# Merging halves of an attention block's PV sums in SBUF by VectorE or GpSimd, with the instruction order searched anew

## The chip, the cores and the metric

One Trainium2 chip, one core of it. The metric is the device time of one execution in microseconds (us). The kernel before took 420.92 us, the median of three runs (420.01 to 422.0).

## The reference

The input x has 2048 rows of 448 numbers in bfloat16. With `xn` the layer norm of x, the kernel computes

```python
s = attention(xn)            # qkv = xn @ wqkv, 16 heads of 28, softmax(q k^T / sqrt(28)) v, then @ wo
g = silu(gelu(xn @ w1 + b1) @ w2 + b2)      # 448 -> 1792 -> 448
return x + s * g
```

The largest part is the softmax: 16 heads with 2048 x 2048 scores each, 67 million exponentials.

## The kernel before, in words

**Tiles.** Heads are taken in 4 groups of four, queries in 4 chunks of 512; a group and a chunk make one of 16 blocks. A block has 16 key tiles of 128 and 4 heads, so 64 positions; there are 1024 positions in all. One position is a score matmul of 128 keys by 512 queries into one of the 8 banks of PSUM (`ring`), with 28 + 4 rows of contraction, so that up to four positions stand in the four row groups of the PE array at the same time (`t_score`, L1680). The PV product of one position is a matmul with 32 output columns; four stand side by side (`t_pv`, L2192) and add up in one bank that is held for the block. A set of four side by side is called a step below.

**Two ways to an exponential.** ScalarE (ACT) takes most positions: one ACTIVATE over two neighbouring banks (a pair, 1024 columns) or three (a triple, 1536), L1734. Some groups of four positions, called late groups, go to VectorE (DVE): one multiply-add and a cast to uint16 make a bfloat16 that is a rough exponential (`p_apass`, L2014, four of 512 columns). To make it finer, two shifted copies are derived from the 2048 columns so obtained (`p_expq`): by one 2048-column DVE instruction each (L2087), or by two halves on GpSimd (POOL, L2081). The three together go through PV, the first with the weights `vaug`, the two copies with scaled weights `vs`. So a late group costs 4 + 4 + 4 matmuls of PV, three steps.

**Merging.** Where the tuning says so (MG), the two copies are added first, so that PV needs two steps, not three, and one buffer comes free early. Before, this is an accumulating DMA in SBUF, issued by GpSimd (L2093).

**Beside the softmax.** The projections for K, Q and V and the first MLP product (L124 with the tile `xnT`) are done in PE's spare time; at the middle ACT changes to the gelu (L1570) and back; after it come the second MLP product, tanh for silu (L1607) and the output projection with `wo` (`p_out`, `p_last`). The sums of the softmax go over DRAM to a reciprocal on GpSimd (L2268) or DVE, back by broadcast, and GpSimd scales the block (L2279). Groups of instructions without effect on the output (the tile `zero`, L124) keep PE busy where the plan sees it idle.

**What sets the order.** There is no order written by hand. A planner (`run`, `put`) has generators for all parts, gives each candidate an estimated start from its own table of durations, priorities and due times, and emits the earliest of each engine. Every engine's program is that list, with semaphore waits where a tile needs another engine. 33 numbers per block (`BP`, read by `tune` when a block's scores begin) steer it: among others S4, R3 and JMAX (how many positions a score set takes), MG, GQ and GE (merging), PS and PQ (shifts on GpSimd), LQ and ND4 (late groups in flight). `NQ` bounds the late groups of a block. A small change of a number moves all that comes after it.

Of the kernel before, what the change touches and what calls it, by code (L numbers as in the profile page):

```python
# [8 lines left out]
ALU = mybir.AluOpType  # L9
ET = mybir.EngineType  # L10

PE, ACT, DVE, POOL, SP = ET.PE, ET.Activation, ET.DVE, ET.Pool, ET.SP
# [17 lines left out]
GM = 582  # L30
BPN = ('S4', 'QF', 'MG', 'GQ', 'GE', 'EPS', 'HP', 'JIT', 'RM', 'RG', 'WT', 'PV0', 'PVC', 'MP', 'ND4', 'LU', 'JOINT', 'LQ', 'JMAX', 'DQ', 'URG', 'SLACK', 'UR', 'QLEAD', 'QDIST', 'R3', 'CN', 'CS', 'SR', 'PS', 'PQ', 'BN', 'PVB')
BP = (
# [17 lines left out]
)  # L50
NQ = (14, 3, 13, 4, 5, 11, 15, 16, 8, 15, 8, 9, 8, 11, 8, 10)
QLEAD, QDIST = 0, 12
JMAX, DQ, LQ, ND4, LU = 2, 3, 2, 3, 3
PV0, PVC, MP = 12, 4, 0.3
# [7 lines left out]
MG, GQ, GE = 1, 4.0, 12  # L62
# [3 lines left out]
TXB = 14  # L66
# [3 lines left out]
GP, MP4, GL = 4.64, 1, 1.2  # L70
JIT, RM, RG, HP = 0.01, 0.1, 0.5, 1.15
URG = 12
SPR, AHEAD = 5, 97
R3 = 0
DUE, UR, M0, M2 = 15, 1.25, 59, 981
VT = (15, 14, 13, 12, 11, 10, 9, 8)
SM_SCALE = DH ** -0.5
LOG2E = 1.4426950408889634
# [12 lines left out]
for i in range(ND):  # L91
    k = F0 // ND + (i < F0 % ND)
# [51 lines left out]
class _Kernel:  # L144
# [1685 lines left out]
    def p_late(self):  # L1830
# [6 lines left out]
        for b in range(NBLK):  # L1837
            i = 0
            while True:
                if i:  # L1840
                    K.nq_read = b
                at = 64 * b - QLEAD + (i * (64 - QDIST) // NQ[b] if i else 0)
                yield ("until", lambda: K.next_m >= at)
                K.nq_read = b
                if i >= NQ[b]:
                    break
# [210 lines left out]
    def p_expq(self, m0, u):  # L2057
        K = self
        b = K.sub_of(m0)
        yield ("until", lambda: K.ln2e == 0 and K.a_left[m0] == 0 and K.unit_of(b, 2 if not any(K.sub_of(x) < b for x in K.pend_q) else 4) is not None)  # L2060
        K.ln2e = 1
        K.need -= 1
        K.pend_q.remove(m0)
        us = [u]
        for _ in range(2):
            v = K.unit_of(b, flat=True)
            K.free_u.remove(v)
            us.append(v)
        u16 = dt.uint16
        bT = K.b_U[u]  # L2070
        for i in (1, 2):
            W, T, bW = *K.pair(us[i], u), K.b_U[us[i]]
            if PS in (i, 3) and K.tE[POOL] < K.now + PQ:
                n = (W.shape[1] if len(W.shape) == 3 else 1024) // PH
                for h in range(PH):
                    sl = slice(n * h, n * h + n)

                    def fs(eng, W=W.bitcast(dt.int32), T=T.bitcast(dt.int32), i=i, sl=sl):
                        w, x = (W[:, sl, :], T[:, sl, :]) if len(W.shape) == 3 else (W[:, sl], T[:, sl])
                        k = K.shc[:, i - 1:i] if len(w.shape) == 2 else K.shc[:, i - 1:i, None]  # L2080
                        return eng.tensor_tensor(w, x, k.to_broadcast(list(w.shape)), ALU.add)  # L2081
                    q = slice(4 // PH * h, 4 // PH * h + 4 // PH)
                    yield _Task(POOL, fs, bT[q] + [K.b_shc], bW[q], PD / PH, 0.05, 2, port=True)
                    K.ln2e = 0
                K.ln2e = 0 if i == 2 else 1
                continue
            yield _Task(DVE, lambda eng, W=W, T=T, i=i: eng.tensor_scalar(W.bitcast(u16), T.bitcast(u16), float(SH[i]), None, op0=ALU.add),  # L2087
                        bT, bW, 0.69, 0.0, 4, port=True)
        K.ln2e = 0
        if MG and not {16, 17, 18} & set(us[1:]) and K.next_m < min(64 * (m0 // 64 + 1) - GE, 64 * TXB) and K.tE[POOL] < K.now + GQ and K.smalls <= K.now + 0.5:  # L2090
            v, w = us[1:]
            W, X = K.unit[v], K.unit[w]
            yield _Task(POOL, lambda eng: eng.dma_start(W, X, accum_op=ALU.add), K.b_U[v] + K.b_U[w], K.b_U[v], TXI, TXL, 2, tx=True)  # L2093
            K.free_u.append(w)
            K.n_mg += 1
            K.late_ready.append((m0, ((u, 0), (v, 1))))
            return
        K.late_ready.append((m0, ((us[0], 0), (us[1], 1), (us[2], 1))))
# [298 lines left out]
```

## Time and profile before

| | before |
|---|---|
| median of three runs | 420.92 us |
| the profiled execution, its own time | 418.29 us |
| its span, first to last instruction | 416.5 us |
| outside the span | 1.8 us |
| granted TensorE clock, mean | 0.995 |

The profile is of one execution. Busy time of an engine is the union of its instructions, and consecutive ACTIVATEs overlap at their ends, so that the distance from start to start says more than a duration. In rows of groups, the columns are line, engine, operation, tiles and shape, count, then busy time and mean duration, then the engine's idle time ahead of them and what ended it. DVE is VectorE, ACT is ScalarE, POOL is GpSimd, SP issues most DMAs.

### The profile page before, as it was taken

The page shows a single profiled execution, that of the slowest core. Times are in us where ns is not written, and L with a number is a line of the kernel's source. Part 1 is how long each engine was busy: PE and PEld are TensorE (multiplying, and loading weights), DVE is VectorE, ACT ScalarE, POOL GpSimd, SP SyncE. Part 2 cuts the span into 40 slices and gives each one's busy share as a digit, 9 for nine tenths or more (in the row PEclk, how much of TensorE's full clock was granted, in tenths as well). Part 3 has the DMA queues.
Part 4 walks back from the last instruction along what each step waited for, and adds up shares of the span by engine and source line. Part 5 has one row for each costly group of instructions (what it writes and reads, how often), then busy time and mean ns, then how long its engine had stood idle before and what let it go on. Part 6 is the DMA issues. An engine that isn't in the chain of part 4 may idle for free.

```text
span 416.5 us, 14489 instructions
## 1 busy us (share of the span) xinstructions
PE 396.2 (95%) x6075; PEld 144.2 (35%) x6075; DVE 345.5 (83%) x603; ACT 402.3 (97%) x414; POOL 175.4 (42%) x197
## 2 busy tenths in 40 slices
PE   6999999999999999999999999999999999999994
PEld 4543233333333232222324443332333333222442
DVE  7958978998888978998998117969988979889676
ACT  5899999999999999999999999999999999999994
POOL 7494692304376484113132401048174053164540
PEclk9999999999999999999999999999999999999998
DMA  8701110100101002101330000341200121010172
GB/s 270 266 4 39 4 32 2 32 2 15 31 4 31 5 28 53 33 3 31 88 98 6 28 4 19 64 77 32 54 3 32 31 54 56 20 29 2 27 156 73
DMA packets 18927, 19.12 MB, mean 46 GB/s; under 512 B 8957, under 2 KB 15181, under 8 KB 18830
## 3 DMA queue, kind: packets, MB, share of 16 engines
q1 hardware_dynamic: 17134, 13.44, 11.1%
q0 software_dynamic: 1440, 4.06, 5.4%
q8 instruction: 48, 0.79, 0.7%
q10 hardware_dynamic: 288, 0.69, 0.5%
q14 instruction: 17, 0.14, 0.1%
HBM read 12.54 MB, written 2.88 MB: 37 GB/s over the span
## 4 chain that ended last, share of the span: by engine, by line
PE 68%; ACT 18%; issue 7%; DVE 6%; POOL 1%; ACTq 0%; POOLq 0%; DVEq 0%
PE ring L124 30%; PE ring L1680 18%; PE ring L2192 16%; ACT P L1734 11%; ACT h L1734 4%; ACT xnT L1734 2%; PE ring L1254 1%; DVE vaug L2014 1%; DVE st L997 1%; PE ring L1494 1%; PE ring L1103 1%; DVE h L1618 1%; ACT w L1607 0%; PE ring L1070 0%; PE ring L1185 0%
## 5 line engine op out<-in xcount | busy, mean ns | idle before, releaser
L1734 ACT ACTIVATE P<-ring 128x1024 bf16<-128x1024 f32 (+1 forms) x245 | 251.3, 1136 | 2.2 <-PE ring L1680 1.3
L1680 PE MATMUL ring<-qT,kT 32*128 32x512 bf16 (+2 forms) x1127 | 132.7, 358 | 6.4 <-ACT P L1734 2.6
L1734 ACT ACTIVATE h<-ring 128x1024 bf16<-128x1024 f32 (+1 forms) x82 | 84.2, 1131 | 0.3
L1680 PEld LDWEIGHTS ring<-qT,kT 32*128 32x128 bf16 x1127 | 36.2, 91 | 120.0 <-ACT P L1734 58.6
L2014 DVE TENSOR_SCALAR vaug<-ring 128x512 uint16<-128x512 f32 x88 | 57.8, 683 | 5.7 <-PE ring L1680 5.2
L124 PE MATMUL ring<-xnT,w 128*32 128x512 bf16 x860 | 57.4, 381 | 1.0 <-DVE h L1506 0.6
L124 PE MATMUL ring<-w,h 128*32 128x448 bf16 x896 | 54.4, 355 | 0.5 <-DVE vaug L2014 0.3
L2192 PE MATMUL ring<-P,vaug 128*32 128x512 bf16 (+2 forms) x609 | 51.3, 354 | 0.6 <-ACT xnT L1734 0.3
L2268 POOL TENSOR_TENSOR rc<-rs,mone 128x16 f32<-128x16 bf16 x11 | 33.9, 3086 | 35.0 <-DMA rs<-E_sb 26.5
L2279 POOL TENSOR_TENSOR qT<-x_sb,E_sb 128x512 bf16<-128x512 f32 x15 | 17.8, 1184 | 57.7 <-DMA x_sb<-recs 20.1
L1734 ACT ACTIVATE xnT<-ring 128x1024 bf16<-128x1024 f32 (+2 forms) x33 | 38.4, 1197 | 0.2 <-PE ring L1680 0.2
L2014 DVE TENSOR_SCALAR x_sb<-ring 128x512 uint16<-128x512 f32 x52 | 34.6, 682 | 2.6 <-PE ring L1680 2.4
L124 PEld LDWEIGHTS ring<-xnT,w 128*32 128x32 bf16 x860 | 20.1, 96 | 27.1 <-issue 6.1
L124 PEld LDWEIGHTS ring<-w,h 128*32 128x32 bf16 x896 | 18.5, 95 | 23.0 <-issue 12.4
L1402 POOL TENSOR_TENSOR qsq<-qT 128x512 bf16<-128x512 bf16 x12 | 12.4, 1037 | 30.1 <-DVE qT L1396 28.6
L2192 PE MATMUL ring<-h,vaug 128*32 128x512 bf16 x202 | 22.9, 384 | 0.0
L2014 DVE TENSOR_SCALAR w<-ring 128x512 uint16<-128x512 f32 x32 | 21.2, 682 | 1.0 <-PE ring L1680 0.5
L1121 DVE CAST kT<-ring 128x512 bf16<-128x512 f32 x11 | 7.6, 688 | 16.6 <-PE ring L124 16.6
L2192 PEld LDWEIGHTS ring<-P,vaug 128*32 128x32 bf16 x609 | 14.3, 95 | 14.8 <-issue 8.0
L2014 DVE TENSOR_SCALAR kT<-ring 128x512 uint16<-128x512 f32 x24 | 15.8, 682 | 4.2 <-PE ring L1680 4.2
L2014 DVE TENSOR_SCALAR h<-ring 128x512 uint16<-128x512 f32 x28 | 18.6, 683 | 0.6 <-PE ring L1680 0.4
L1612 POOL TENSOR_TENSOR h<-w 128x448 bf16<-128x448 bf16 x12 | 12.4, 1033 | 15.0 <-PE ring L124 10.0
(235 smaller groups left out, 626.2 us busy)
## 6 DMA issues: line engine op xcount, KB each, us to landing
x_sb<-recs SPq DMA_DIRECT2D x60, 64.0 KB, 2.0
w<-in_B_w_dram SPq DMA_DIRECT2D x1, 1568.0 KB, 7.5
w<-in_B_w_dram SPq DMA_DIRECT2D x1, 1344.0 KB, 8.4
kT<-kT POOLq DMA_DIRECT2D x2, 512.0 KB, 5.5
x_sb<-in_A_x_dram SPq DMA_DIRECT2D x2, 448.0 KB, 4.6
out_dram<-in_A_x_dram SPq DMA_DIRECT2D x2, 448.0 KB, 10.3
out_dram<-h POOLq DMA_DIRECT2D x4, 224.0 KB, 5.1
out_dram<-h SPq DMA_DIRECT2D x8, 112.0 KB, 3.5
```

The costliest lines, as they stand in the source:

```text
L124: ins = eng.matmul(out[q:q + 32, :], w[:, q:q + 32], x, tile_position=(0, q), start=start, stop=stop, skip_group_check=True)
L997: yield _Task(DVE, lambda eng, i=i, t=t: eng.bn_stats(K.st6[:, i, :], K.x_sb[:, c, t, :]), [K.b_x0[h] if c == 0 else K.b_x[c]], [K.b_st[c] ...
L1103: return eng.matmul(bank, w[sl, 3, g * 128:(g + 1) * 128], K.xnT[sl, 3, c * 512:(c + 1) * 512], tile_position=pos, start=False, stop=True, ...
L1121: fn = lambda eng: eng.tensor_copy(dst, bank)
L1402: yield _Task(POOL, lambda eng: eng.tensor_tensor(qs, qb, qb, ALU.mult), [qr], [tq], 1.1, 0.05, 2, port=True)
L1612: yield _Task(POOL, lambda eng, o=o, t=t: eng.tensor_tensor(o, sg[:, t, :], fb[:, t, :], ALU.mult), [K.b_sig[c % 2], K.b_fsb[c % 2]], [K.b ...
L1680: return eng.matmul(dst, K.kT[32 * j:32 * j + 32, g, t * 128:(t + 1) * 128], K.qT[32 * j:32 * j + 32, g, c * 512 + q0:c * 512 + q0 + nq], ...
L1734: return eng.activation(reg[:, i0:i0 + n, :], src, ACTF.Exp, scale=SM_SCALE)
L2014: yield _Task(DVE, lambda eng: eng.tensor_scalar(K.part(u, k).bitcast(dt.uint16), K.like(u, bank), SM_SCALE * LOG2E * 128.0, (127.0 - EXP_ ...
L2192: return eng.matmul(acc[32 * j:32 * j + 32, q0:q0 + nq], w, ap[:, col:col + nq] if len(ap.shape) == 2 else ap[:, col // 128:(col + nq) // ...
L2268: yield _Task(POOL, lambda eng: eng.tensor_tensor(K.rc[:, :], K.rs[:, :], K.mone[:, 0:1].to_broadcast([128, 16]), ALU.pow), [K.b_srs, K.b_ ...
L2279: yield _Task(POOL, lambda eng: eng.tensor_tensor(dst, K.rb, E, ALU.mult), [K.b_rb, tE], [K.b_onT[g][c]], 1.15, 0.05, 1, port=True)
```

## The change

A second branch for merging is put ahead of the old one: for MG = 2 the two copies of a late group are added by one DVE instruction of 2048 columns, for MG above 2 by four GpSimd instructions of 512. The old condition becomes MG == 1. The numbers of the plan are replaced: 16 of the 17 rows of `BP`, `NQ`, `AHEAD`, `M0` and `M2`. In the new rows MG is 2 in one row (the third block's), 1 in seven and 0 in nine; none is above 2.

```diff
-NQ = (14, 3, 13, 4, 5, 11, 15, 16, 8, 15, 8, 9, 8, 11, 8, 10)
+NQ = (14, 4, 4, 4, 7, 10, 15, 16, 8, 15, 11, 9, 5, 9, 8, 10)
...
-SPR, AHEAD = 5, 97
+SPR, AHEAD = 5, 89
...
-DUE, UR, M0, M2 = 15, 1.25, 59, 981
+DUE, UR, M0, M2 = 15, 1.25, 62, 984
...
-        if MG and not {16, 17, 18} & set(us[1:]) and K.next_m < min(64 * (m0 // 64 + 1) - GE, 64 * TXB) and K.tE[POOL] < K.now + GQ and K.smalls <= K.now + 0.5:
+        if MG > 1 and not {16, 17, 18} & set(us[1:]) and K.next_m < 64 * (m0 // 64 + 1) - GE and K.tE[DVE if MG == 2 else POOL] < K.now + GQ:
+            v, w = us[1:]
+            W, X = K.unit[v], K.unit[w]
+            if MG == 2:
+                yield _Task(DVE, lambda eng: eng.tensor_tensor(W, W, X, ALU.add), K.b_U[v] + K.b_U[w], K.b_U[v], 1.15, 0.0, 4, port=True)
+            else:
+                for k in range(4):
+                    yield _Task(POOL, lambda eng, y=K.part(v, k), z=K.part(w, k): eng.tensor_tensor(y, y, z, ALU.add),
+                                [K.b_U[v][k], K.b_U[w][k]], [K.b_U[v][k]], 1.16, 0.05, 2, port=True)
+            K.free_u.append(w)
+            K.n_mg += 1
+            K.late_ready.append((m0, ((u, 0), (v, 1))))
+            return
+        if MG == 1 and not {16, 17, 18} & set(us[1:]) and K.next_m < min(64 * (m0 // 64 + 1) - GE, 64 * TXB) and K.tE[POOL] < K.now + GQ and K.smalls <= K.now + 0.5:
```

Counted in the two programs as they are built (line numbers of the kernel before):

| | before | after |
|---|---|---|
| ACT exponentials: pairs, triples, singles | 298, 61, 1 | 264, 84, 0 |
| late groups | 61 | 61 |
| of these in blocks 0 to 15 | 1 3 6 3 4 2 5 5 3 4 4 5 4 5 5 2 | 1 4 3 3 4 4 4 4 4 4 5 6 4 4 5 2 |
| merges: by DMA, by DVE, by GpSimd | 6, 0, 0 | 3, 2, 0 |
| shifts: DVE of 2048, GpSimd halves | 101, 42 | 92, 60 |
| score sets on PE (one to four positions at once) | 372 | 355 |
| PV matmuls of 512 columns | 1408 | 1412 |
| matmuls of the tile `zero` | 36 | 96 |
| output tiles that take the way over ACT at the end (L2301) | 0 | 1 |

The 17 score sets fewer hold the same number of positions. The first block has the same counts in both.

32 rows, old and new, of the table BP are left out of this document.

## Prediction

> **What bounds the kernel now.** I read the page first, its span and its first part.
>
> ```profile
> span 416.5 us, 14489 instructions
> PE 396.2 (95%) x6075; PEld 144.2 (35%) x6075; DVE 345.5 (83%) x603; ACT 402.3 (97%) x414; POOL 175.4 (42%) x197
> ```
>
> ACT and PE both look full. To tell which one sets the pace I asked for what ACT waits for, and for its busy time in two long stages that hold little but exponentials, with the groups that make them up.
>
> ```profile
> ACT P L1734 <- PE ring L1680: 1.3, 2, 0.8
> ACT P L1734 <- PE ring L2192: 0.4, 1, 0.4
> ACT xnT L1734 <- PE ring L1680: 0.2, 1, 0.2
> ...
> 40.00:220.00 180.00, 179.66 (x186) 1.00 0.12 29
> 252.00:400.00 148.00, 146.47 (x138) 1.00 0.17 38
> ...
> L1734 ACT ACTIVATE P<-ring 128x1024 bf16<-128x1024 f32 x98 | 94.8, 1084 | 0.1
> L1734 ACT ACTIVATE h<-ring 128x1024 bf16<-128x1024 f32 x66 | 65.6, 1080 | 0.1
> L1734 ACT ACTIVATE P<-ring 128x1536 bf16<-128x1536 f32 x12 | 17.9, 1496 | 0.0
> L1734 ACT ACTIVATE h<-ring 128x1536 bf16<-128x1536 f32 x10 | 15.0, 1498 | 0.1
> ```
>
> The first three lines are who ended ACT's waits ahead of exponentials, with the total, the number and the longest: in the whole span 1.9 us, each time PE. The next two are ACT's busy time in 180 and 148 us; the last four are the groups of the first of these stages. The mean durations overstate the cost, as one ACTIVATE begins before the last ends. The distance of starts is in ACT's timeline, in a place without waits.
>
> ```profile
> 119.79 5.61 ACT L1734 ACTIVATE P<-ring 128x1024 bf16<-128x1024 f32 x6
> 125.23 4.75 ACT L1734 ACTIVATE h<-ring 128x1024 bf16<-128x1024 f32 x5
> ...
> 340.41 1.49 ACT L1734 ACTIVATE xnT<-ring 128x1536 bf16<-128x1536 f32 x1
> 341.74 5.59 ACT L1734 ACTIVATE P<-ring 128x1024 bf16<-128x1024 f32 x5
> ```
>
> Six pairs take 125.23 - 119.79 = 5.44 us, 0.907 each; the triple takes 341.74 - 340.41 = 1.33. The 164 pairs and 22 triples of the first stage then need 148.7 + 29.3 = 178.0 of its 180 us. In the second stage ACT's groups are:
>
> ```profile
> L1734 ACT ACTIVATE P<-ring 128x1024 bf16<-128x1024 f32 x77 | 76.1, 1053 | 0.3
> L1734 ACT ACTIVATE P<-ring 128x1536 bf16<-128x1536 f32 x27 | 39.8, 1489 | 1.1 <-PE ring L1680 0.6 <-PE ring L2192 0.4
> L1734 ACT ACTIVATE xnT<-ring 128x1536 bf16<-128x1536 f32 x12 | 17.6, 1477 | 0.2 <-PE ring L1680 0.2
> L1734 ACT ACTIVATE xnT<-ring 128x1024 bf16<-128x1024 f32 x17 | 17.5, 1058 | 0.0
> L1607 ACT ACTIVATE w<-w 128x1792 bf16<-128x1792 bf16 x3 | 5.2, 1727 | 0.0
> L1607 ACT ACTIVATE w<-w 128x1344 bf16<-128x1344 bf16 x1 | 1.3, 1336 | 0.0
> L1575 ACT ACT_TABLE_LOAD x1 | 1.3, 1283 | 0.0
> ```
>
> 94 x 0.907 + 39 x 1.33 + 7.8 = 144.9 of 148 us. So ACT sets the pace; all that a better order can win in these 328 us is 2.0 + 3.1 = 5.1 us, and the change gives ACT the same 780 positions. PE is second: it is what ACT's few waits end with.
>
> **ACT's own work.** 34 pairs and one single become 23 triples. Before: 298 x 0.907 + 61 x 1.33, and about 0.5 for the single (between nothing and a pair), 351.9 us. After: 264 x 0.907 + 84 x 1.33 = 351.2. That is **-0.7**, on the path.
>
> **The merges.** Six accumulating transfers become three, and two additions on DVE come in; the GpSimd branch is never taken, as no row of the table has MG above 2. The rows that price these:
>
> ```profile
> L2093 POOL DMA_DIRECT2D kT<-kT x2: 927/1048/1170, 258.1 to 272.3; - x2
> DMA to landing us min/median/max: 4.5/4.8/6.4
>   DVE x_sb L2087: 0.8, 1
> ...
> L1404 DVE TENSOR_TENSOR qsq<-qT x3: 415/424/425, 32.3 to 43.6; 128x512 bf16<-128x512 bf16 x3
> L2309 DVE TENSOR_TENSOR h<-h x8: 381/392/394, 401.6 to 413.9; 128x448 bf16<-128x448 bf16 x8
> L2014 DVE TENSOR_SCALAR x_sb<-ring x52: 620/680/692, 51.5 to 349.4; 128x512 uint16<-128x512 f32 x52
> ```
>
> The third line is who waited for a transfer: one DVE instruction, 0.8 us, once. DVE isn't the bound, so three transfers fewer give between 0 and -0.8 on the path; I take 0. An addition of 2048 columns isn't in the trace: by the slope from 448 to 512 columns (32 ns for 64) it is 0.42 + 24 x 0.032 = 1.2 us, an estimate, at most four times the 512 row, 1.7. Behind each stands a late pass (L2014) of the next group, which then gives back its bank up to 1.2 us late, and PE waits for that bank if it needs it. By the number of exponentials ahead of them (66 and 72, at about 0.93 us each from the 30th at 40 us, an estimate) the two fall at some 75 to 80 us, where DVE is nearly full in this trace (14.74 of 15 us busy):
>
> ```profile
> 75.00:90.00 15.00, 14.74 (x27) 1.00 0.09 23
> ```
>
> What covers them is that this block now has three late groups instead of six: at four passes of 0.68 and two shifts each, some 4 us of DVE a group. I cost them at 0; without that cover they would cost 2.4, and what each can win besides, its saved PV step, is 0.2. One merge fewer in all is one PV step more, 0.2 us of PE.
>
> **DVE, POOL and PE otherwise.** Nine shifts of 0.68 leave DVE (-6.2), two additions come (+2.4), with one partial sum fewer some -4.5 of 345.5. POOL gets 18 halves more:
>
> ```profile
> L2081 POOL TENSOR_TENSOR x_sb<-w,shc x6: 1037/1037/1039, 58.5 to 136.3; 128x512 int32<-128x512 int32 x6
> L2081 POOL TENSOR_TENSOR kT<-vaug,shc x6: 1037/1037/1887, 140.0 to 388.4; 128x512 int32<-128x512 int32 x6
> L2087 DVE TENSOR_SCALAR qsq<-vaug x2: 679/1004/1328, 308.9 to 345.6; 128x2048 uint16<-128x2048 uint16 x2
> L2087 DVE TENSOR_SCALAR x_sb<-vaug x16: 675/683/1021, 203.7 to 371.8; 128x2048 uint16<-128x2048 uint16 x16
> ...
> 144.22 0.39 PE L1680 MATMUL ring<-qT,kT 32*128 32x512 bf16 x3
> 144.55 0.40 PE L2192 MATMUL ring<-P,vaug 128*32 128x512 bf16 x4
> 144.77 0.39 PE L2192 MATMUL ring<-h,vaug 128*32 128x512 bf16 x4
> 145.09 0.40 PE L1680 MATMUL ring<-qT,kT 32*128 32x512 bf16 x4
> ```
>
> 18 x 1.04 = 18.7 us on an engine that is 42% busy, less three issues of 1.05. The PE lines price a step at 144.77 - 144.55 = 0.22 us and a set of scores at 0.33 (144.22 to 144.55), whether it holds three or four. Seventeen sets fewer are -3.7 (at a step's price) to -5.6 us of PE; three steps more (one PV, one lone late score, one projection remainder) +0.7. The extra `zero` groups run where the plan has PE idle, and cost nothing while that holds; five more groups of three steps of a quarter length are under 1 us of PE otherwise. So PE is lighter by some 3 to 5 of 396 us.
>
> What that brings is not in a row. PE ends every visible wait of ACT, so part of the 5.1 us of gaps should go, between 0 and 5.1. Against it: ACT's idle time ahead of triples in the second stage is 1.3 for 39, 33 ns each, ahead of pairs 0.3 for 94, 3 ns. 23 triples more at 33 ns and 34 pairs fewer at 3 are +0.7. I take a net of **-0.6**, of a possible -5.1 to +0.7, near the small end because in the first stage the gaps are already only 1%.
>
> **The end.** After the last exponential the two programs differ:
>
> ```profile
> 407.32 2.45 ACT L1734 ACTIVATE xnT<-ring 128x1024 bf16<-128x1024 f32 x3
> ...
> 410.60 0.28 ACT L2221 ACTIVATE E_sb<-ring 128x128 bf16<-128x128 f32 x1 [0.37 <-PE ring L2192]
> 410.93 0.24 PE L124 MATMUL ring<-E_sb,selb 128*32 128x128 bf16 x4 [0.38 <-ACT E_sb L2221]
> ```
>
> The last exponential ends at 407.32 + 2.45 = 409.8, 6.7 us ahead of the span's end. After, 16 matmuls with `wo` (four steps of 0.22, 0.9 us) stand on PE between the last PV and the last `selb`, where PE now sits idle 0.4 us for ACT's copy; that can delay the reciprocal by up to 0.5. One output tile more is finished here: a multiplication more on DVE (0.39, the L2309 row) near the last output. Both only add, so nothing is won; hidden they cost 0, in full 0.9. I take **+0.3**, since the DVE part has slack beside the wait for PE.
>
> **Sum.** -0.7 - 0.6 + 0.3 = -1.0 against the profiled execution's 418.29: 417.3. Its median of three is 420.92, 2.6 above; there the forecast is **419.9 us**, practically no change. A measurement of this kernel can tell about 0.5% (2.1 us) from none.
>
> **Rivals.**
> - *Most of the gaps close.* The order was searched, and all three loaded engines have less to do. If four fifths of the 5.1 us go: -0.7 - 4.1 + 0.3 = -4.5, 416.4. For it: every named ACT wait is PE's, and PE gets lighter. Against it: the gaps are small and many, 16 ns on the mean of 319 exponentials.
> - *Slower: triples starve the ring.* A triple needs three adjacent banks of eight; with the next unit's scores five or six are bound, and PV sums, projections and late passes share the rest. Its place is the stretches dense with triples, and it decides once every tenth triple waits as long as the largest wait in the rows above for a score, 0.8: 8 x 0.8 = 6.4, less the 1.3 that is there now, 5.1; with the other terms +4.7, 425.6. For it: 33 ns against 3 ns. Against it: in the same stage PE loses sets. A late pass behind a merge or a POOL half feeds the same wait.
> - *Shifts and halves block each other.* One half took 1.89 instead of 1.04, one shift 1.33 instead of 0.68. Three such in the rows above, each one of its group, make 18 more halves cheap; if each stretched one shift by 0.65, DVE had 11.7 us more, more than the 4.5 it saves, and where DVE is full about a third would show: 418.29 + 3.9 - 1.0 = 421.2, on the median 423.8. [...]
> - *The change does hardly what it says*: five merges in place of six, and the new branch twice. That is certain from the counts, so all difference comes from the order; taken alone it is 0, 420.9.
>
> **How the numbers follow.** Forecast 0.45 (418.2 to 421.8 by its terms, with -2.0 for the gaps as the border to the first rival), gaps close 0.22, ring starved 0.2, blocking 0.08, no difference at all 0.05. Faster by over 0.5% is below 418.8: the second case and a sixth of the first, 0.3. Slower is above 423.0: third and fourth case and a little of the first, 0.3. Within: 0.4. The range, 416.4 to 425.0, leaves out the better half of the first rival and the worse half of the second, 0.1 each.
>
> **What would show it.** ACT's stage sums: about 351 us of distances for 264 pairs and 84 triples, as counted; named waits of ACT for PE at 1 to 4 us (under 1 speaks for the first rival, over 6 for the second); additions L2094 of 1.2 us with no PE wait behind them; DVE busy near 341, POOL near 191; shifts with a median of 0.68 and few above 1; from the last exponential to the end 6.7 us and up to 0.9 more. It is wrong if the startup, whose instructions are the same in both, or the gelu stage changes its length, or if waits on DVE or POOL appear in ACT's list.

## The result, and the profile after

The changed kernel takes 417.72 us (median of 6 runs, 417.02 to 418.41). The kernel before, run beside it again, has 420.41 (6 runs, 419.13 to 422.0). The medians lie 2.7 us apart; the ratio on record is 0.9949, with a 95% interval of 0.9925 to 0.9973: some 2.1 us faster, between 1.1 and 3.2. The forecast was 1.0 us faster and 419.9. The time lies inside the range, but 0.5 below the forecast's own terms (418.2 to 421.8), between them and the first rival's 416.4. The kernel before itself came out 0.5 below the 420.92 from which the forecast was reckoned.

The profiled executions differ less: 417.02 against 418.29, 1.3 us, in the spans too. First the page of the changed kernel, the span and the engines' busy time.

```profile
span 415.2 us, 14613 instructions
PE 393.5 (95%) x6144; PEld 143.6 (35%) x6144; DVE 343.3 (83%) x595; ACT 402.0 (97%) x403; POOL 188.1 (45%) x212
```

PE is 2.7 us lighter (3 to 5 were forecast), DVE 2.2 (4.5), GpSimd 12.7 heavier (15.6), ACT the same within 0.3. Now the same two stages of ACT as before: busy time in them, then the groups of the first stage, then those of the second that hold exponentials.

```profile
40.00:220.00 180.00, 179.44 (x178) 1.00 0.11 26
252.00:400.00 148.00, 146.69 (x136) 1.00 0.16 36
...
L1734 ACT ACTIVATE P<-ring 128x1024 bf16<-128x1024 f32 x82 | 82.7, 1110 | 0.1
L1734 ACT ACTIVATE h<-ring 128x1024 bf16<-128x1024 f32 x58 | 60.1, 1097 | 0.4 <-PE ring L2205 0.3
L1734 ACT ACTIVATE P<-ring 128x1536 bf16<-128x1536 f32 x23 | 35.4, 1540 | 0.0
L1734 ACT ACTIVATE h<-ring 128x1536 bf16<-128x1536 f32 x15 | 22.8, 1522 | 0.0
...
L1734 ACT ACTIVATE P<-ring 128x1024 bf16<-128x1024 f32 x61 | 60.5, 1044 | 0.6 <-PE ring L2205 0.3
L1734 ACT ACTIVATE P<-ring 128x1536 bf16<-128x1536 f32 x33 | 48.2, 1478 | 0.7 <-PE ring L1680 0.4
L1734 ACT ACTIVATE xnT<-ring 128x1024 bf16<-128x1024 f32 x26 | 26.5, 1050 | 0.0
L1734 ACT ACTIVATE xnT<-ring 128x1536 bf16<-128x1536 f32 x11 | 16.2, 1477 | 0.0
```

With 0.907 us a pair and 1.33 a triple, 140 pairs and 38 triples are 177.5 of 180 us; 87 and 44, with the same 7.8 us of tanh and table load as before, are 145.2 of 148. The gaps are 2.5 + 2.8 = 5.3 us, where they were 5.1. The two stages are as tight as they were.

Where the 1.3 us of the spans lie is told by the first and the last exponential. The next rows are the line's instructions that write P, with first and last start, of the kernel before and of the changed one; then the changed kernel's end.

```profile
L1734 ACT ACTIVATE P<-ring x245: 1005/1072/1607, 13.6 to 406.4; 128x1024 bf16<-128x1024 f32 x106, 128x1536 bf16<-128x1536 f32 x17
```

```profile
L1734 ACT ACTIVATE P<-ring x229: 1004/1085/1697, 13.0 to 407.0; 128x1024 bf16<-128x1024 f32 x84, 128x1536 bf16<-128x1536 f32 x31
...
406.97 1.03 ACT L1734 ACTIVATE P<-ring 128x1024 bf16<-128x1024 f32 x1
408.82 0.28 ACT L2234 ACTIVATE E_sb<-ring 128x128 bf16<-128x128 f32 x1 [0.36 <-PE ring L2205]
409.35 0.24 PE L124 MATMUL ring<-E_sb,selb 128*32 128x128 bf16 x4
```

| us | before | after | difference |
|---|---|---|---|
| first exponential begins | 13.6 | 13.0 | -0.6 |
| from there to the end of the last one | 396.2 (to 409.8) | 395.0 (to 408.0) | -1.2 |
| from there to the end of the span | 6.7 | 7.2 | +0.5 |

The first row is not the change: the instructions there are the same in both programs, and the start moves between executions (an experiment below began at 15.3). What the order does is -1.2 + 0.5 = -0.7 in this pair of executions.

The traces tell further where the -1.2 lies. From the first exponential to the table load of the gelu both take the same (211.1 and 211.0 us), and so does the gelu stage (27.1 in both). From there to the end of the last exponential it is 157.9 before and 156.8 after: the difference stands in the second half.

### The profile page after: what moved, and what is told of

Read it like the earlier page. It is cut to its first block, busy times and chain, and to the rows that moved or that the text cites. A ratio compares the mean times of both kernels' runs of the same rounds, so it can differ in the third digit from the quotient of the medians.

```text
span 415.2 us, 14613 instructions
## 1 busy us (share of the span) xinstructions
PE 393.5 (95%) x6144; PEld 143.6 (35%) x6144; DVE 343.3 (83%) x595; ACT 402.0 (97%) x403; POOL 188.1 (45%) x212
## 4 chain that ended last, share of the span: by engine, by line
PE 65%; DVE 13%; ACT 13%; issue 5%; DMA 1%; POOL 1%; DVEq 0%; ACTq 0%; POOLq 0%
PE ring L124 32%; PE ring L1680 17%; PE ring L2205 14%; ACT P L1734 7%; ACT h L1734 5%; DVE vaug L2014 2%; DVE x_sb L2014 2%; DVE st L997 1%; PE ring L1494 1%; DMA x_sb<-in_A_x_dram 1%; ACT xnT L1734 1%; DVE x_sb L2087 1%; DVE kT L2087 1%; DVE h L2087 1%; DVE E_sb L2267 1%
## 5 line engine op out<-in xcount | busy, mean ns | idle before, releaser
L1734 ACT ACTIVATE P<-ring 128x1024 bf16<-128x1024 f32 (+1 forms) x229 | 247.3, 1186 | 1.5 <-PE ring L1680 0.4
L1680 PE MATMUL ring<-qT,kT 32*128 32x512 bf16 (+2 forms) x1126 | 128.9, 359 | 6.4 <-ACT P L1734 1.9
L2014 DVE TENSOR_SCALAR vaug<-ring 128x512 uint16<-128x512 f32 x92 | 61.2, 683 | 7.6 <-PE ring L1680 5.6
L2205 PE MATMUL ring<-P,vaug 128*32 128x512 bf16 (+2 forms) x600 | 53.1, 352 | 1.0 <-ACT P L1734 0.4
L1734 ACT ACTIVATE xnT<-ring 128x1024 bf16<-128x1024 f32 (+1 forms) x40 | 45.1, 1168 | 0.5 <-PE ring L1680 0.5
L2014 DVE TENSOR_SCALAR w<-ring 128x512 uint16<-128x512 f32 x52 | 34.7, 685 | 2.7 <-PE ring L1680 2.1
L2014 DVE TENSOR_SCALAR x_sb<-ring 128x512 uint16<-128x512 f32 x40 | 26.3, 681 | 2.4 <-PE ring L1680 1.6
L2205 PE MATMUL ring<-h,vaug 128*32 128x512 bf16 x193 | 22.7, 383 | 0.5 <-ACT P L1734 0.4
L1396 DVE CAST qT<-ring 128x512 bf16<-128x512 f32 x15 | 10.3, 689 | 15.3 <-PE ring L124 14.9
L1612 POOL TENSOR_TENSOR h<-w 128x448 bf16<-128x448 bf16 x12 | 12.4, 1036 | 20.9 <-DMA qpad<-qT 13.3
L2205 PEld LDWEIGHTS ring<-P,vaug 128*32 128x32 bf16 x600 | 15.9, 96 | 16.2 <-issue 7.4
L1508 DVE CAST h<-ring 128x512 bf16<-128x512 f32 x24 | 16.4, 688 | 5.0 <-PE ring L124 4.9
L1402 POOL TENSOR_TENSOR qsq<-qT 128x512 bf16<-128x512 bf16 x12 | 12.5, 1039 | 17.8 <-DVE qT L1396 17.8
L124 PE MATMUL ring<-xnT,wk 128*32 128x512 bf16 x232 | 17.9, 383 | 0.0
```

The costliest lines, as they stand in the source:

```text
L124: ins = eng.matmul(out[q:q + 32, :], w[:, q:q + 32], x, tile_position=(0, q), start=start, stop=stop, skip_group_check=True)
L1396: yield _Task(DVE, lambda eng: eng.tensor_copy(qb, bank), [tok], [qr], 0.7, 0.0, dp)
L1402: yield _Task(POOL, lambda eng: eng.tensor_tensor(qs, qb, qb, ALU.mult), [qr], [tq], 1.1, 0.05, 2, port=True)
L1508: yield _Task(DVE, lambda eng: eng.tensor_copy(dst, bank), [tok], wr, 0.69, 0.0, 2)
L1612: yield _Task(POOL, lambda eng, o=o, t=t: eng.tensor_tensor(o, sg[:, t, :], fb[:, t, :], ALU.mult), [K.b_sig[c % 2], K.b_fsb[c % 2]], [K.b ...
L1680: return eng.matmul(dst, K.kT[32 * j:32 * j + 32, g, t * 128:(t + 1) * 128], K.qT[32 * j:32 * j + 32, g, c * 512 + q0:c * 512 + q0 + nq], ...
```

## The experiments

**The theories.** A: ScalarE sets the pace, so the time follows the floor of its exponentials (0.907 a pair, 1.33 a triple), and the merges cost and win nothing, since VectorE and the transfers have cover. M: the merging itself is the gain, by fewer late transfers. S, later P: TensorE is the pace, or matched with ScalarE. O: the order as such, not its counts, decides. The first five runs keep the order and change sizes in place. The others change a setting, and the order is made anew. The kernel before took 418.7 us (25 runs) on the chip of the first four runs, 418.4 and 419.1 (7 runs each) in the two later sets. Times are compared by the ratio to it.

**The additions on VectorE.** A quarter of each of the two additions is left; part of two merges is left out.

```diff
-                yield _Task(DVE, lambda eng: eng.tensor_tensor(W, W, X, ALU.add), K.b_U[v] + K.b_U[w], K.b_U[v], 1.15, 0.0, 4, port=True)
+                yield _Task(DVE, lambda eng, y=K.part(v, 0), z=K.part(w, 0): eng.tensor_tensor(y, y, z, ALU.add), K.b_U[v] + K.b_U[w], K.b_U[v], 1.15, 0.0, 4, port=True)
```

> The changed kernel with the same order; the two additions on VectorE take only 512 of their 2048 columns (part of two merges is left out). That is 2 x (1.21 - 0.42) = 1.6 us less of VectorE in the third block. Theory A (ScalarE sets the pace, the additions are hidden): no change to the changed kernel, 417.7 within 0.5. Theory M (the merge itself has a price on the path): up to 1.6 faster, 416.1.

Measured: 417.08 us (11 runs), ratio 0.9959 (0.9944 to 0.9975). The changed kernel has 0.9949 (0.9925 to 0.9973). No gain: the additions are hidden, as A says; M's full 1.6 us is outside the intervals. As the order is the changed kernel's, this run also measures it a second time, on another chip and beside 25 runs of the kernel before: about 1.7 us faster.

**The accumulating transfers.** In the kernel before, each of the six takes a quarter of its columns; part of six merges is left out.

```diff
-            yield _Task(POOL, lambda eng: eng.dma_start(W, X, accum_op=ALU.add), K.b_U[v] + K.b_U[w], K.b_U[v], TXI, TXL, 2, tx=True)
+            yield _Task(POOL, lambda eng, y=K.part(v, 0), z=K.part(w, 0): eng.dma_start(y, z, accum_op=ALU.add), K.b_U[v] + K.b_U[w], K.b_U[v], TXI, TXL, 2, tx=True)
```

> The kernel before with the same order; the six accumulating transfers take only 512 of 2048 columns (part of six merges is left out), so they land earlier than the 4.5 to 6.4 us of the trace. Theory A: no change to the kernel before, ratio 1.000 within 0.002. Theory M (late transfers were what cost the kernel before its time, and the change won by having three instead of six): 1.0 to 2.7 us faster, ratio 0.994 to 0.998, and less scatter between runs.

Measured: 419.15 us (12 runs, 417.69 to 421.27), ratio 1.0004 (0.9988 to 1.0021). Neither the time nor the scatter moved. What the change spared in transfers is worth nothing here; M falls. Both runs price what a merge costs. What it saves, a PV step and a buffer, wasn't varied in place; the run with TensorE shortened, below, bounds the steps.

**ScalarE shortened in place.** A sixteenth of each exponential from the 61st instruction on is left out.

```diff
-            def fexp(eng, src=K.span(ids), reg=reg, i0=i0, n=n):
+            q = 480 if u >= 60 else 512
+
+            def fexp(eng, src=K.span(ids)[:, :, 0:q], reg=reg[:, :, 0:q], i0=i0, n=n):
```

> The changed kernel with the same order; from the 61st exponential instruction on, ScalarE takes 480 of each 512 columns (the rest of P is left stale). Some 657 banks x 32 columns x 0.83 ns = 17.5 us less of ScalarE, nothing else changed. Theory A: ScalarE sets the pace, so at least half of it shows, 9 to 17 us faster (400 to 409). Rival S (TensorE's stream is the pace, ScalarE only looks full): under 4 us faster (over 413.7).

Measured: 413.54 us, ratio 0.9870 (0.9841 to 0.9898), 3.7 us below the run with the same order above (0.0089 of 418.7; by the medians 3.5). The 17.5 us is an estimate by columns (0.83 ns each: a triple's 1.33 less a pair's 0.907, over 512); ACT's busy time falls by 12.2, from 402.0 to 389.8, as the profile's page says:

```profile
PE 391.0 (95%) x6144; PEld 143.1 (35%) x6144; DVE 343.2 (83%) x595; ACT 389.8 (95%) x403; POOL 188.1 (46%) x212
```

By either number less than a third of it shows: A's "at least half" is wrong, S's "under 4" is met. ACT's list of waits says what came up: this is the shortened kernel, and then the changed one.

```profile
ACT P L1736 <- PE ring L1680: 4.3, 18, 0.5
ACT xnT L1736 <- PE ring L1680: 1.3, 3, 0.9
ACT h L1736 <- PE ring L1680: 0.7, 3, 0.3
```

```profile
ACT xnT L1734 <- PE ring L1680: 0.5, 1, 0.5
ACT P L1734 <- PE ring L1680: 0.4, 2, 0.2
```

Visible waits for scores go from 3 to 24. So in this order the time follows ACT for only some 4 us; then ACT waits for PE's scores.

**TensorE shortened in place.** The PV matmuls of the finer copies take a quarter of the queries; the rest of these sums is left out.

```diff
                 i = K.vt[g].index(t) if v else 0
+                nq = min(nq, 128) if v else nq
                 w = K.vs[:, g % 2, i, j, :] if v else K.vaug[:, t, 4 * g + j, :]
```

> The changed kernel with the same order; the PV matmuls with the weights vs take 128 of 512 columns (three quarters of the two finer copies are left out of the sums). 117 steps x 0.165 = some 19 us less of TensorE, ScalarE unchanged. Theory A: only gaps can go, 0 to 5 us faster (412.7 to 417.7). Rival S: at least half of 19 shows, 9 us or more (under 408.7).

Measured: 416.23 us (7 runs), ratio 0.9942 (0.9922 to 0.9963): 0.7 us less than the same order above, within the intervals. By the estimate (three quarters of a step's 0.22 us, 117 times) some 19 us of PE are gone; its busy time, a union in which four short matmuls still last 0.23 us where four full ones last 0.40, falls by 11.5 (from 393.5 to 382.0), and the time is the same. So S falls as well: PE alone isn't the pace. And the two copies' PV steps, of which a merge spares one, are worth next to nothing in time.

```profile
PE 382.0 (92%) x6144; PEld 142.6 (34%) x6144; DVE 344.2 (83%) x595; ACT 401.3 (96%) x403; POOL 188.1 (45%) x212
```

This profiled execution took 417.98; its first exponential begins late, at 15.3:

```profile
L1734 ACT ACTIVATE P<-ring x229: 1006/1092/1742, 15.3 to 407.9; 128x1024 bf16<-128x1024 f32 x84, 128x1536 bf16<-128x1536 f32 x31
```

That is the 2.3 us of startup (13.0 in the changed kernel) by which an execution of one and the same stretch of instructions can differ, more than the whole change in these profiles.

**Both shortened.** The two edits together.

> The changed kernel with the same order and both cuts of the earlier runs: ScalarE takes 480 of each 512 columns from the 61st exponential on (17.5 us less), and the PV matmuls with vs take 128 of 512 columns (some 19 us less of TensorE). Apart they gave 3.5 and about 1 us. If the two engines are matched and take turns as the pace (rival P), together they give much more than the sum, 8 us or more (under 409). If something else stands behind both (VectorE, the order of waits), together they give the sum or little more, 4 to 6 (411 to 413).

Measured: 409.74 us, ratio 0.9782 (0.9743 to 0.9821), 7.4 us below the same order uncut; the sum of the two alone is 3.7 + 0.7 = 4.4. That is more than the sum by 3.0 us (uncertain by some 2, an estimate from the intervals), so the two engines do cover each other; less than "8 or more", so something else stands close behind. ACT is short by 17.5 us of work and the time by 7.4. The trace shows where the remaining 10 us are: in small gaps between exponentials. The shortened pairs start 0.85 us apart at the least and 0.94 on the mean; what lies beyond the least, for pairs and triples together, is 20.1 us here and 10.2 in the changed kernel. What rules these gaps stays open. ACT's named waits for PE are 5.8 us for scores and 1.1 for PV, and the longest waits of PE's weight loads (45.2 us in all) are for banks that ACT holds, so each waits for the other; no run tells that loop from a third engine.

**The new numbers without the new branch.** `BP`, `NQ`, `AHEAD`, `M0` and `M2` of the changed kernel are put into the kernel before; one line is shown.

```diff
-NQ = (14, 3, 13, 4, 5, 11, 15, 16, 8, 15, 8, 9, 8, 11, 8, 10)
+NQ = (14, 4, 4, 4, 7, 10, 15, 16, 8, 15, 11, 9, 5, 9, 8, 10)
```

> The kernel before with the new numbers of the plan and without the new branch, so that MG = 2 means an accumulating transfer again; the order is made anew. Built, it has 269 pairs, 83 triples, one single, 59 late groups, 375 score sets and 7 merges, all by transfer. Theory A (ScalarE's exponentials are the floor: time follows 0.907 us a pair and 1.33 a triple): 354.9 against 351.2 of the changed kernel, so 3.7 slower than it, 420.8 where it takes 417.1. Theory O (fine order and chance of the search decide, counts don't): anywhere within 2 of it. Theory M (the branch itself brings the gain): as the kernel before, 418.7.

Measured: 432.9 us, four runs from 426.04 to 435.16, too far apart for a ratio. It is at least 7 us slower than the kernel before, so all three expectations fail; A's floor is 3.0 us above the kernel before's, the smaller part of it.

**No merges.** `MG` is 0 in all rows; one row is shown.

```diff
-    (4, 1, 2, 2.679, 7, 0.183, 1, 0.096, 0.306, 0.455, -0.495, 13, 1, 0.532, 2, 8, 0.101, 4, 1, 11, 9, 0.691, 0.7, 68, 14, 1, 0, 2.474, 3, 2, 5.685, 22, 3.0),
+    (4, 1, 0, 2.679, 7, 0.183, 1, 0.096, 0.306, 0.455, -0.495, 13, 1, 0.532, 2, 8, 0.101, 4, 1, 11, 9, 0.691, 0.7, 68, 14, 1, 0, 2.474, 3, 2, 5.685, 22, 3.0),
```

> The changed kernel with MG = 0 in all rows, so no late group is merged; the order is made anew. Built: 281 pairs, 75 triples, one single, 59 late groups, 385 score sets. Theory A: floor 355.1, 3.9 above the changed kernel's, 421.0. Theory M (merging pays by itself): more than that, as five merges are five PV steps (1.1 us of TensorE) on top. Theory O: within 2 of 417.1.

Measured: 436.48 us, ratio 1.0433 (1.0419 to 1.0448), 18 us slower than the kernel before. The five merges are worth 1.1 us of PE, and A's floor is 3.2 us above the kernel before's; the size says that most of the cause is elsewhere. One place is plain in the timeline. The columns are start, duration, engine, line, tiles, and what the engine idled for; the last four rows are stretches of 5 us with the busy time of PE, PEld, DVE, ACT and GpSimd, the granted clock, the DMA share and GB/s.

```profile
205.01 0.40 SPq L923 DMA_DIRECT2D w<-in_B_w_dram  x1
205.51 0.91 SPq L1908 DMA_DIRECT2D qpad<-qT  x1
212.61 0.62 PE L124 MATMUL ring<-qpad,kT 128*32 128x512 bf16 x4 [4.01 <-DMA qpad<-qT]
...
205.00:210.00 5.00, 3.56 (x50) 1.10 (x46) 3.24 (x5) 4.79 (x6) 2.09 (x7) 1.00 0.76 226
210.00:215.00 5.00, 2.39 (x22) 0.54 (x22) 1.30 (x3) 0.34 (x1) 2.53 (x1) 0.61 0.35 102
215.00:220.00 5.00, 5.00 (x38) 0.72 (x30) 2.74 (x5) 3.53 (x4) 0.38 (x1) 0.50 0.16 43
220.00:225.00 5.00, 4.32 (x53) 1.12 (x49) 3.89 (x7) 4.33 (x6) 0.00 (x0) 0.87 0.06 21
```

In this order the fetch of the padded queries (32 KB) is issued half a microsecond behind the load of the second MLP weight (1568 KB). It lands 7.1 us later, PE stands still for 4.0 us with its lone late score at the head of its queue, and ACT works 0.34 of the next 5 us. Then the granted clock (the third column from the right) falls to 0.61, 0.50 and 0.87, and the stop is paid a second time by slow matmuls: the four behind it take 0.62 us, where four of the same shape, at 207.9 us, took 0.40. In the changed kernel the same fetch is issued 4 us ahead of the load:

```profile
198.27 0.55 SPq L1908 DMA_DIRECT2D qpad<-qT  x1
202.27 0.40 SPq L923 DMA_DIRECT2D w<-in_B_w_dram  x1
```

**A constant that means nothing to the chip.** One entry of the plan's durations is moved by a thousandth of a microsecond, up and down, in the changed kernel.

```diff
-SEM, OWN, SEMW = 0.07, 0.03, 0.15
+SEM, OWN, SEMW = 0.071, 0.03, 0.15
```

> The changed kernel with the same tables; one constant of the plan's table of durations (a semaphore's latency) is 0.071 instead of 0.07, which means nothing for the chip but makes the order anew. Built: 271 pairs, 82 triples, 59 late groups, 354 score sets, 8 merges. Theory A: floor 354.9, so 3.7 slower than the changed kernel, 420.8, though TensorE has one score set fewer. Theory O: within 2 of 417.1.

> As the other run with a meaningless constant, here 0.069 instead of 0.07. Built: 286 pairs, 72 triples, 59 late groups, 366 score sets, 5 merges (3 by transfer, 2 on VectorE, as in the changed kernel). Theory A: floor 355.2, 4.0 slower than the changed kernel, 421.1. Theory O: within 2 of 417.1.

Measured: 440.08 us, ratio 1.0512 (1.0487 to 1.0538), and 429.15, ratio 1.0231 (1.0201 to 1.0262). 21 and 10 us slower than the kernel before, by a constant without meaning. A's floor explains 3.0 and 3.3 of it (3.7 and 4.0 against the changed kernel). The first of the two even has fewer score sets than the changed kernel (354) and more merges (8), so the counts on which part of the prediction rested don't rank orders. In its list two rows alone hold 15.5 us in which exponentials wait for PE, where the changed kernel's list has 1.5 in all (the 0.5 and 0.4 above, and twice 0.3 for the ring's L2205):

```profile
ACT P L1734 <- PE ring L1680: 9.1, 9, 3.5
ACT P L1734 <- PE ring L2205: 6.4, 3, 2.5
```

**The same for the kernel before**, with 0.075.

> The kernel before with the meaningless constant at 0.075 instead of 0.07. Built: 267 pairs, 86 triples, 58 late groups, 369 score sets, 6 merges. Theory A: floor 356.6 against 351.9, 4.7 slower than the kernel before, ratio 1.011. Theory O: ratio within 0.995 to 1.005. If both searched kernels lose by a meaningless change, the search had picked each for its own order, and a comparison of the two is one of two picks.

Measured: 427.36 us, ratio 1.0177 (1.0135 to 1.0219), 7.4 us slower where A says 4.7. So, as far as three draws can tell, both kernels are picked orders, and an order that the same planner makes without a pick loses 7 to 21 us.

**No triples.** R3 is 0 in all rows; one row is shown.

```diff
-    (4, 1, 2, 2.679, 7, 0.183, 1, 0.096, 0.306, 0.455, -0.495, 13, 1, 0.532, 2, 8, 0.101, 4, 1, 11, 9, 0.691, 0.7, 68, 14, 1, 0, 2.474, 3, 2, 5.685, 22, 3.0),
+    (4, 1, 2, 2.679, 7, 0.183, 1, 0.096, 0.306, 0.455, -0.495, 13, 1, 0.532, 2, 8, 0.101, 4, 1, 11, 9, 0.691, 0.7, 68, 14, 0, 0, 2.474, 3, 2, 5.685, 22, 3.0),
```

> The changed kernel without triples (R3 = 0 in all rows); the order is made anew. Built: 384 pairs, 64 late groups, 402 score sets, 7 merges. Theory A: the floor is 348.3, 2.9 below the changed kernel's, 414.2, if TensorE keeps up. Rival P (TensorE is matched with ScalarE, as the shortened exponentials suggest: 17.5 us less of ScalarE gave 3.5): 47 sets more at 0.33 to 0.43 us are 15 to 20 us of TensorE, and the kernel is 3 or more slower, over 420.

Measured: 426.55 us, ratio 1.0190 (1.0166 to 1.0215), 8 us slower than the kernel before. P's direction holds. The profile shows how it comes about:

```profile
span 424.3 us, 14588 instructions
...
L1734 ACT ACTIVATE P<-ring x259: 1006/1046/1210, 13.7 to 408.9; 128x1024 bf16<-128x1024 f32 x130
414.22 0.54 ACT L2314 ACTIVATE h<-ring 128x448 bf16<-128x448 f32 x1 [3.09 <-PE ring L124]
418.01 0.54 ACT L2314 ACTIVATE h<-ring 128x448 bf16<-128x448 f32 x1 [0.21 <-PE ring L124]
```

The last exponential begins at 408.9 and lasts 1.1 us; the span ends 14.3 us after it (7.2 in the changed kernel): the floor sank by 2.9, gaps took it back, and PE reached the end with output tiles undone, six of which go over ACT there. Work that PE can't fit beside the exponentials comes out at the end.

**GpSimd merges.** MG is 3 in the third block, the branch that the change has and doesn't use.

```diff
-    (4, 1, 2, 2.679, 7, 0.183, 1, 0.096, 0.306, 0.455, -0.495, 13, 1, 0.532, 2, 8, 0.101, 4, 1, 11, 9, 0.691, 0.7, 68, 14, 1, 0, 2.474, 3, 2, 5.685, 22, 3.0),
+    (4, 1, 3, 2.679, 7, 0.183, 1, 0.096, 0.306, 0.455, -0.495, 13, 1, 0.532, 2, 8, 0.101, 4, 1, 11, 9, 0.691, 0.7, 68, 14, 1, 0, 2.474, 3, 2, 5.685, 22, 3.0),
```

> The changed kernel with MG = 3 in the third block, so that GpSimd merges there (the branch that the change has and does not use); the order is made anew. Built: 264 pairs, 85 triples, one single, 60 late groups, 370 score sets, 7 merges: 5 by transfer, 2 on GpSimd (four of 512 columns each). Theory A: floor 353.0, 1.8 slower than the changed kernel, 418.9. Theory M: GpSimd's halves delay VectorE's shifts and the late groups, so more than 1 beyond that, over 420.

Measured: 431.68 us, ratio 1.0295 (1.0264 to 1.0326). By number this is M's side, but it shows nothing of GpSimd: the order is new from that block on, and it lies among the other orders made without a pick (427 to 440). What a merge on GpSimd costs in a fixed order wasn't tried.

**What sets the slowest draws apart.** Of the six orders made anew whose runs agree among themselves, three have a mean granted clock of 0.98 to 0.99: no merges (436.5 us), the constant moved up (440.1) and GpSimd merges (431.7). The other three have 0.99 or more and take 426.6 to 429.2. Ahead of the last 15 us of the profiles the clock is at half for 10.2, 13.7 and 13.7 us in the first three, for 0 to 3.4 in the others, and never in the two picked orders. The half clock came without one long stop, too. With GpSimd merges and with the constant moved up, PE is busy for about half of 5 us, no single stop longer than 1 us, and the stretch behind runs at half clock, 0.50 (columns as above):

```profile
210.00:215.00 5.00, 2.35 (x26) 0.69 (x22) 4.25 (x7) 5.00 (x7) 1.90 (x7) 0.96 0.92 294
215.00:220.00 5.00, 3.67 (x27) 0.76 (x27) 3.35 (x6) 4.75 (x5) 3.55 (x3) 0.50 0.03 4
```

```profile
205.00:210.00 5.00, 2.65 (x28) 0.62 (x24) 4.03 (x7) 5.00 (x5) 3.56 (x7) 0.95 0.70 221
210.00:215.00 5.00, 4.18 (x38) 1.15 (x39) 1.38 (x2) 4.51 (x4) 2.59 (x2) 0.50 0.03 5
```

How much of the loss is the clock's and how much the stops' ahead of it, no run separates.

No run beat the changed kernel at full work.

## Why the prediction was right, and where it was off

- *ACT is the bound, and the change leaves its work.* The second half held; the first only for some 4 us. With some 19 us less on PE the time stays (0.9942 against 0.9959), so PE alone isn't the pace. But with some 17.5 us less on ACT only 3.7 show, and with both cut 7.4: the next limit stands 4 us behind ACT, and PE's work is only part of it. Where the prediction says that PE is "what ACT's few waits end with", it had the clue and drew too little from it.
- *-0.7 for ACT's floor, -0.6 for gaps.* From the first to the last exponential the profiles differ by 1.2 us; the sum was 1.3. The split can't be told so finely: the gaps in the two long stages went from 5.1 to 5.3, not down, so the -0.6 for gaps isn't borne out there: what makes up the 1.2 beside the floor, 0.7 us, lies in the stages around them. That the sum comes out at 1.2 is in part luck.
- *Merges at 0.* Their own cost is shown by the two runs in place. The addition takes what was worked out, 1.2 us:

```profile
L2094 DVE TENSOR_TENSOR x_sb<-x_sb x1: 1215/1215/1215, 76.7 to 76.7; 128x2048 bf16<-128x2048 bf16 x1
L2094 DVE TENSOR_TENSOR h<-h x1: 1214/1214/1214, 82.8 to 82.8; 128x2048 bf16<-128x2048 bf16 x1
  POOL qT L2292: 2.3, 1
```

  Only GpSimd waited for one of them (the last line), once. The place, 77 and 83 us, is the one that was estimated.
- *The end at +0.3.* +0.5 measured. The step of PE is seen in the end's rows: ACT's copy is done at 408.82 + 0.28 = 409.1, and the matmul with `selb` starts at 409.35, 0.25 later, where it started 0.05 later before. The further multiplication on DVE is the rest.
- *First rival, gaps close.* No; they stayed, though the time, 417.7, came nearer to its 416.4 than to the forecast. *Second rival, triples starve the ring.* No: ahead of 44 triples in the second stage ACT idles 0.7 us, 16 ns each, where it was 33. *Third, shifts and halves block each other.* All 60 halves take 1.03 to 1.04 us. A few shifts are stretched, here the groups with the longest; DVE has 2.2 us less to do in all, not 4.5, and no trace of it in ACT's waits. The rows on which the rival stood show something else: in the trace of before no shift overlaps a half at all. The half of 1.89 began inside an instruction on DVE that adds and multiplies (L1618), the shift of 1.33 inside a multiplication on GpSimd (L1612). After, nine shifts take over 0.76 us; two of them (0.76 and 0.96) began inside a half, the other seven inside multiplications and additions on GpSimd (L1402, L1612, L1614).

```profile
L2087 DVE TENSOR_SCALAR kT<-vaug x9: 682/686/1294, 194.2 to 372.3; 128x2048 uint16<-128x2048 uint16 x9
L2087 DVE TENSOR_SCALAR h<-vaug x6: 683/685/1229, 148.2 to 376.5; 128x2048 uint16<-128x2048 uint16 x6
L2087 DVE TENSOR_SCALAR wk<-xnT x2: 684/902/1119, 263.5 to 365.0; 128x2048 uint16<-128x2048 uint16 x2
```

- *The step that was mis-sized* is the price of an order. The prediction let it range over a few us by counts of sets and triples. Four orders of the same tables or nearly the same (the two with the constant moved, the kernel before with it moved, the new numbers without the branch) lie 7 to 21 us above the kernel before, with floors only 3 to 5 higher. That the new order lands some 2 us from the old one can't be read from any count. It fits that both orders were picked, and then the prediction came out near by that luck; no run shows the picking itself.
- *Open:* the order's part in the pair of profiles is 0.7 us, the two ratios give 2.1 (1.1 to 3.2) and 1.7 (1.0 to 2.3). The profiled execution of the kernel before, 418.29, is faster than all six of its timed runs on that chip, so the profiles understate the difference. One more profile of its order, the run with short transfers (418.65 us), begins its exponentials at 13.0 and takes 212.0 us from there to the gelu, against 211.1: a microsecond of gaps comes and goes between executions. Why it does, no run shows.
- *Signs named ahead.* ACT's named waits of exponentials for PE are 1.5 us in all (1 to 4 were forecast), the gelu stage keeps its length, and no exponential waits visibly for DVE or GpSimd.

## What to carry to other kernels

Where a planner or a search writes the order, a change of code is first of all a new draw of the order. Before crediting an operation, change it in place with the order held (a quarter of its columns will do), and move a meaningless constant to see how far draws lie apart: here the operation cost 0 and a draw up to 21 us. Two engines at 95% and more are told apart by shortening each alone and then both: here 3.7, 0.7 and 7.4 us, so neither alone sets the pace, and even both together aren't all of it.

## What the runs showed of the hardware

- A 32 KB fetch issued on the same queue 0.5 us behind a 1568 KB load landed after 7.1 us; the median of the 13 such fetches is 1.8 us.
- PE's stop of 4.0 us came with a granted clock of 0.61, 0.50 and 0.87 in three stretches of 5 us: by these shares it was at half from 211.1 us, 2.5 after the stop began, to 221.3, 8.7 after PE worked again. With GpSimd merges and with the constant moved up the half clock (0.50 in 5 us) came behind 5 us in which PE was busy for 2.35 and 2.65 us, with no single stop longer than 1 us.
- Back to back, pairs and triples start 0.907 and 1.33 us apart, though one lasts 1.07 and 1.49: a triple saves only 1.5 x 0.907 - 1.33 = 0.03 us against one and a half pairs, so fewer and longer exponentials win little on ACT itself.
- A shift on VectorE that began inside a GpSimd multiplication of 1.04 us took 1.33 us instead of 0.68, and a GpSimd half that began inside a VectorE instruction of 1.12 us took 1.89 instead of 1.04.
- The same startup instructions put the first exponential at 13.0 to 15.3 us in the profiled executions. A difference of 1 us between two profiles of this kernel needs that number beside it.
